# S4 convolution times SwiGLU gate on one core: the last two output tiles finished in column halves, their stores on two queues, and the fill of ones put first in the list

## The chip, the core and the metric

One core of one Trainium2 chip. The metric is device microseconds of one execution; a kernel's time is the median of its runs. The kernel before ran three times: 611.83, 613.95 and 614.11 us, median 613.95 us.

## What is computed

The input u has L = 2048 rows of D = 512 columns. It is normalised by row, and from the normalised rows come an S4 convolution over time and a SwiGLU feed-forward network, whose SiLU gates the convolution:

```python
xn = _layernorm(x)                       # x = A_u, (1, 2048, 512)
P  = exp(logdA[:, :, None] * l)          # (512, 128, 2048), complex
K  = einsum("dn,dnl,dn->dl", Cc, P, dB).real
s  = irfft(rfft(xn padded to 4096) * rfft(K padded)) + xn * Dskip
g  = silu((silu(xn @ w_gate) * (xn @ w_up)) @ w_down)     # 512 -> 1792 -> 512
return x + s * g
```

## The kernel before: tasks, a list and a planner

**Tasks.** The kernel is written as 1,964 small tasks. Each call of `add` (line 141) describes one: an engine, a planned duration, a function that emits its instructions, and the buffers that it reads and writes. `LIST` (line 47) is a fixed permutation of the tasks, two characters for each; it is the order in which they are emitted, and so the order of every engine's in-order queue. Loads are issued by SP, most stores to the output by ACT.

**The planner.** `Plan.run` (line 177) walks the list and gives each task a planned start and end from planned durations. It does not change the order. From the planned times come three things. Buffers in on-chip memory get an address in one arena of 118 KB per partition (`place`, line 289): two buffers may share bytes if their planned lives do not meet, and the later one's first writer then waits in fact for the earlier one's last reader. PSUM banks are picked by the earliest planned release. And `keep_warm` (line 254) puts fill matmuls (line 1423) of a constant tile of ones into the PE queue where PE would stand idle by plan: a gap from s to e is filled with `int((e - s - 0.2) * 0.8 / 0.213)` of them, in front of the task that ends the gap; the first gap begins at a fixed 1.5 us. A fourth thing is `part_ports` (line 243), which adds a wait between a DVE task and a later POOL task that the plan puts within 8 us of each other.

**The start.** The first rows of x are loaded in 128-row tiles (`rows_in`, L489), the weights in seven column chunks for each of gate, up and down (`w_load`, issued at L468). A chunk's squares are summed on ACT (L604), cast to the row `hsq` on DVE (L614), summed over partitions by a matmul with the tile of ones (L615), and turned into a scale on DVE (L635 to L639). With the scale ACT makes the f16 high part of the chunk (L669) and DVE the low part (L670). A tile of x has its statistics on DVE (L503), is centred and scaled on ACT (L529, L530), its low part made on DVE (L531), is transposed on PE (L540) and copied from PSUM on DVE (L546). Then the first feed-forward matmuls can run (L699; down projection L741). The first stage of the transform of x is L563, copied by ACT (L567). The constant of ones, with a column of pi/2, is written by the DVE task at L474; before the change it stands 15th in the list, and fifth among DVE's tasks, behind two tiles' statistics, the Newton steps of the reciprocal root and the first `hsq`.

**The end.** `final` (line 1292) finishes the output: for a pair of tiles and one half of the columns it loads the transformed product (L1305, issued at L468), the rows of x (L1309) and the stored gate, does the last matmul (L1324), multiplies by the gate on DVE (L1333), adds x on POOL or, for the last tiles, DVE (L1336, L1338), and ACT stores two 64-row halves (L1340). The last two tiles, 14 and 15, are done singly over all 512 columns; their gate comes straight from the down projection: ACT's SiLU (L748) of a 128x512 PSUM bank.

ACT's queue at the end of the list before, in order: a store of pair 0/1, one of pair 4/5 and one more of 0/1, the two of tile 14 with the two of pair 12/13 (seven stores, between the SiLU of tile 14 and that of tile 15); then the SiLU of tile 15, the two stores of pair 2/3, the two of pair 6/7 and the two of tile 15.

Of the kernel before, what the change touches and what calls it, by code (L numbers as in the profile page):

```python
# [13 lines left out]
I32 = mybir.dt.int32  # L14
AF = mybir.ActivationFunctionType
# [14 lines left out]
NB = 8  # L30
# [17 lines left out]
    "#)#(#'#K#&#%#J#L#.#T#i#M#N#k###l#/#O#U#R#j#m#V#n#1#v#P#2#Q#S#D#Y#4#W#-#X#Z#5#+#w#o#x#y#q#,#p#r#*&+#8#z(*#s#t&.(+"  # L48
# [9 lines left out]
    ".M)e.G%]..)X.-./.L.N*$.X.Q.S.O.P%Z.R)Y)Z.T%[.0.1)m%a._.`%d.f)y'')n.b.3.U.2)z)f)[)o*%){)g%X%i'1.[.^.l.m)h*&.Y)p.a"
    "*'.o*()v.V**.c.|.Z)q%b.])|)r.i.k.n.p.g.h.}/#/$*..j%^/%%e*1)}/&/'/(*#%j.d.q.r%c.s*2//*3%k*)*:%n%f*/%g%s.t&{*0.v%_"
    "/).u*;*+*B*4*C.w%h.x.y.z.{/*/+%o%p*</,/./-*6*D*E/5%t/6/0%q/1/3*,/7%l*-/2/D*5*F*7/8/:/Q/9/>&|%m%r&)*G/</4*>/;/S%u"  # L60
    "*8/@*9%v*=*?/=';/?/E*L&'*M/F/H'%/G*@%w*H*A/R/j/I/k/l/M*N*P*I*J/J/O/K/L*K/i*O%y/N'&/A/B*Q*T*U*V*]/Z/]*X/T/V/X/Y'("
    "*R/[/m/n')/U'**S/W'</P/^*W/C/o/p'2/_*Y*Z'3'=/q*[*h%x/}'+/r/s/`*^'4'5/t/u*o/v*e'E'F'G/a*f*g*i',/c/d'T/e%z&#'6'/%{"
    "/b/f/h/g/y&$*j'9'7*_/{%|'-*k*l'.0U&%*a01/w/x0#&&%}&*/z'>*`*b'?0$'H'I*p0%02*c*q*d*m0&0>*n0+/|0:0<&(0V*w0(0?0X0W0'"
    "*x0Z+$0)+%0[0-*r030*0,'U050B0D0G0Y0^07040I0@0A0C'V0.+.0]'00806'J'M090;0E+/*s0_'@0F0`'N0H*t0/00':'K0=0J0a'S'Y'A'B"
    "+&+''C'D+0*u*v0b0K*y0L0n0c0d0e0g0h0i0k+1+60f*z1/0j0M'q0l0Q'L0p0O0o'Z'O0P0N1#*{0u0v0m+(0r0t0R0S0w0}100q0s*|+)1$+*"
    "0T0y*}+#++0x1G+21H1)1*'R'P1F1J+31K1L1,1I+7+81%1'0z+,+-+:1+1-+4+51315'W181:+911+;12141&1(0{0|'{1617+I19+>+<1M'Q1Q"
    "+=1T1U1O+?+@+A1N'81.'X'['g1[1W']1;1<1P1=+F+G1R'|'}+B+C1>1B1Z1V'^'_1]1^1S1x+D1X1@1_'r'h's'i1A+P1j+Q+X+Y1b1a+a+b't"
# [53 lines left out]
class Plan:  # L121
# [55 lines left out]
    def run(self):  # L177
        order = [self.tasks[i] for i in LIST]
        free = dict.fromkeys(("PE", "DVE", "ACT", "POOL", "SP"), 0.0)
# [3 lines left out]
        dma_free = port_free = 0.0  # L183
# [209 lines left out]
def kernel(  # L393
# [73 lines left out]
    def load(dst, src, names, size, pieces, pr, rd=(), ahead=None):  # L467
        add("SP", 0.4, lambda: sy.dma_start(dst(), src), up=names, rd=rd, pr=pr, dma=dma_us(size, pieces), root=True, ahead=ahead)  # L468
# [260 lines left out]
    def down(b, t, c, hh, pos):  # L729

        idx = (b * 2 + t) * NC + c
        if c == 0:
            zps[b, t] = bank(f"z{b}{t}", "p")
        z = zps[b, t]

        def mm():
            h = hh.view(F16).rearrange("p (l n) -> p l n", l=2)
            w = wt["d"][:, c].rearrange("p l (i d) -> p l i d", i=2)
            for i in range(2):
                for k, (hl, wl) in enumerate(((0, 0), (0, 1), (1, 0))):  # L740
                    T.matmul(z.t, h[:, hl, i * 256 + t * P:i * 256 + (t + 1) * P], w[:, wl, i],  # L741
                             start=(c == 0 and i == 0 and k == 0), stop=(c == NC - 1 and i == 1 and k == 2))
        add("PE", 1.3, mm, rd=[hh, key(f"wd{c}")], wr=[z], up=[key(f"down{idx}")], pr=ffn_due(pos) + W["dn"],
            slack=SLD if b == t == 0 else 0.0)
        if c == NC - 1:
            j = 2 * b + t
            zg = zgs[j] = buf(f"zg{j}", 2048, "zg" if b < ZK else None, 2)
            add("ACT", 0.69, lambda: S.activation(zg.f32(), z.t, AF.Silu, scale=zsc[:, 1:2]), rd=[z], wr=[zg], c=1, pr=0)  # L748
# [7 lines left out]
    def prep(hf):  # L756
# [395 lines left out]
    def kg_s1(i):  # L1152
# [109 lines left out]
    def s2_inv(m, c):  # L1262
# [17 lines left out]
        for q in range(4):  # L1280
# [8 lines left out]
            add("SP", 0.4, lambda q=q, b=b: sy.dma_start(bs_d[c, m, q].rearrange("k p d -> p k d"), b.f32().rearrange("p (k d) -> p k d", k=2)),  # L1289
                rd=[b], up=[key(f"bs{c}")], c=0, dma=dma_us(262144, 256))  # L1290

    def final(js, cs, c):
# [33 lines left out]
        add("PE", 0.92 if nj == 2 else 1.06, mm, rd=[bt, key("j2")], wr=[py], c=2, pr=pr, f32=6)  # L1326
        ot = buf(f"ot{tag}", 2048, "ot", int(W["c_ot"] + 0.5))
# [24 lines left out]
    add("SP", 0.4, lambda: sy.dma_start(ldt, log_dt.rearrange("(c p) -> p c", p=P)), up=[key("ldt")], pr=18, dma=0.7)  # L1352
# [4 lines left out]
    for k in range(2):  # L1357
        add("SP", 0.4, lambda k=k: sy.dma_start(dsk[k * 64:k * 64 + 64].rearrange("(f r) d -> f r d", r=2)[:, k], dskip.partition_broadcast(32)),
# [112 lines left out]
```

## Time and profile before

| | |
|---|---|
| three runs | 611.83, 613.95, 614.11 us; median 613.95 |
| the profiled execution | 610.76 us; its span 609.0 us, so 1.76 us lie around the span |
| PE busy | 581.9 us, 96% of the span |
| DVE, ACT, POOL busy | 432.3, 342.1, 326.2 us |
| moved by DMA | 93.10 MB |

Times in the views are microseconds from the start of the span. A line of the timeline gives start, duration, engine, source line, operation, tiles and shapes, how often it came in a row, and in brackets how long the engine had stood idle and what released it. PE is the matmuls, PEld the weight loads beside them; SPq and ACTq are DMA issues on those engines' queues.

### The profile page before, as it was taken

How to read it: one execution, taken by the hardware profiler on the slowest of the kernel's cores; microseconds unless marked ns; L12 is line 12 of the kernel's file. 1: busy time of each engine (PE TensorE's matmuls, PEld its weight loads, DVE VectorE, ACT ScalarE, POOL GpSimd, SP SyncE). 2: the span in 40 equal slices, each digit the busy share in tenths (PEclk: the TensorE clock that was granted, in tenths of full speed). 3: DMA queues.
4: the chain of work that ended last, by engine and by line, in shares of the span. 5: the costliest groups of instructions: out<-in, count | busy, mean ns of one | idle time of the engine just before them, and what ended most of it. 6: DMA issues, size and time to landing. Idle time of an engine off the chain costs nothing.

```text
span 609.0 us, 18323 instructions
## 1 busy us (share of the span) xinstructions
PE 581.9 (96%) x7625; PEld 411.6 (68%) x7625; DVE 432.3 (71%) x988; ACT 342.1 (56%) x697; POOL 326.2 (54%) x301
## 2 busy tenths in 40 slices
PE   4999999999999999999999999999989999999974
PEld 1678886556888678766787677776657656667531
DVE  3777989665798989888779876878848556673313
ACT  5689856655765468667778687746632423131100
POOL 0145522279974768649997799688023341530131
PEclk9999999999999999999999999999989999999978
DMA  8699621024004041025340123556969889999997
GB/s 261 167 286 321 196 79 48 1 97 155 16 3 95 4 113 37 2 68 169 114 110 15 30 79 138 172 129 172 320 180 275 265 246 270 270 286 255 222 265 184
DMA packets 100594, 93.10 MB, mean 153 GB/s; under 512 B 38496, under 2 KB 83808, under 8 KB 100512
## 3 DMA queue, kind: packets, MB, share of 16 engines
q1 hardware_dynamic: 96000, 87.48, 50.0%
q10 hardware_dynamic: 4512, 4.46, 2.8%
q8 instruction: 60, 0.98, 0.7%
q14 instruction: 22, 0.18, 0.1%
HBM read 59.02 MB, written 32.90 MB: 151 GB/s over the span
## 4 chain that ended last, share of the span: by engine, by line
PE 84%; DMA 9%; DVE 3%; issue 1%; ACT 1%; SPq 0%; ACTq 0%; POOL 0%; DVEq 0%; POOLq 0%
PE p L699 45%; PE p L741 21%; PE p L1145 5%; DMA out_dram<-arena 3%; PE p L1230 3%; PE p L1237 2%; DMA arena<-zg_d 2%; DMA arena<-in_A_u_dram 2%; PE p L1277 2%; PE p L563 2%; PE p L1423 2%; PE p L1178 1%; DMA arena<-bs_d 1%; PE p L540 1%; DMA wd<-in_B_w_gate_dram 1%
## 5 line engine op out<-in xcount | busy, mean ns | idle before, releaser
L699 PE MATMUL p<-arena,wu 128*128 128x256 f16 x1344 | 157.3, 274 | 4.0 <-issue 4.0
L741 PE MATMUL p<-wd,arena 128*128 128x512 f16 x672 | 155.4, 381 | 0.0
L699 PE MATMUL p<-arena,wg 128*128 128x256 f16 x1344 | 155.2, 273 | 0.0
L699 PEld LDWEIGHTS <-wu 128*128 128x128 f16 x1344 | 130.7, 98 | 26.9 <-issue 8.8
L699 PEld LDWEIGHTS <-wg 128*128 128x128 f16 x1344 | 129.7, 98 | 23.0 <-issue 3.7
L741 PEld LDWEIGHTS <-arena 128*128 128x128 f16 x672 | 63.5, 98 | 77.1 <-issue 9.3
L1078 POOL TENSOR_TENSOR arena<-arena 128x1536 f32<-128x1536 f32 x32 | 90.7, 2840 | 18.0 <-DVE arena L854 5.6
L720 ACT ACTIVATE arena<-p,inv 128x512 f32<-128x512 f32 x56 | 38.4, 689 | 65.4 <-PE p L699 57.1
L1070 POOL TENSOR_TENSOR arena<-arena 128x1024 int32<-128x1024 int32 x32 | 62.4, 1955 | 18.5 <-DVE arena L830 7.5
L722 DVE SCALAR_TENSOR_TENSOR p<-p,shc,arena 128x512 f32<-128x512 f32 x56 | 42.2, 754 | 30.1 <-PE p L699 17.8
L724 ACT CAST arena<-p 128x512 f16<-128x512 f32 x56 | 32.5, 589 | 33.8 <-DVE p L722 16.4
L1113 DVE TENSOR_TENSOR arena<-arena,p 128x512 f32<-128x512 f32 x64 | 43.6, 681 | 8.4 <-ACT p L1094 6.4
L1336 POOL TENSOR_TENSOR arena<-arena 128x512 f32<-128x512 f32 x12 | 15.1, 1268 | 57.7 <-DMA arena<-in_A_u_dram 37.9
L725 DVE TENSOR_TENSOR arena<-p,arena 128x512 f16<-128x512 f32 x56 | 37.7, 683 | 11.2 <-ACT arena L724 11.2
L1094 ACT ACTIVATE p<-p,halfpi 128x512 f32<-128x512 f32 x64 | 42.4, 664 | 1.4
L1093 ACT ACTIVATE p<-arena 128x512 f32<-128x512 int32 x64 | 38.9, 610 | 6.4 <-DVE arena L1185 2.2
L1095 ACT ACTIVATE p<-arena 128x512 f32<-128x512 int32 x64 | 37.5, 602 | 8.7 <-DVE arena L1115 4.5
L1259 POOL TENSOR_TENSOR arena<-arena 128x512 f32<-128x512 f32 x16 | 20.3, 1275 | 38.5 <-DVE arena L1255 14.1
L1260 POOL TENSOR_TENSOR arena<-arena 128x512 f32<-128x512 f32 x16 | 20.3, 1272 | 31.3 <-DVE arena L1255 17.8
L1119 DVE SCALAR_TENSOR_TENSOR arena<-arena,p 128x256 f32<-128x256 f32 x64 | 26.5, 414 | 12.6 <-ACT p L1095 8.9
L1145 PEld LDWEIGHTS p<-arena 128*32 128x32 f32 x2048 | 29.7, 110 | 6.6 <-issue 4.2
L1145 PE MATMUL p<-arena 128*32 128x64 f32 x2048 | 33.4, 220 | 0.0
(180 smaller groups left out, 814.0 us busy)
## 6 DMA issues: line engine op xcount, KB each, us to landing
ax_d<-arena SPq DMA_DIRECT2D x32, 256.0 KB, 2.6
ak_d<-arena SPq DMA_DIRECT2D x16, 512.0 KB, 6.5
arena<-ak_d SPq DMA_DIRECT2D x16, 512.0 KB, 5.7
arena<-ax_d SPq DMA_DIRECT2D x16, 512.0 KB, 6.7
bs_d<-arena SPq DMA_DIRECT2D x32, 256.0 KB, 4.8
arena<-in_A_u_dram SPq DMA_DIRECT2D x62, 128.0 KB, 5.0
arena<-in_B_w_down_dram SPq DMA_DIRECT2D x14, 512.0 KB, 6.0
arena<-bs_d SPq DMA_DIRECT2D x14, 512.0 KB, 8.5
```

What stands on the lines that cost most here:

```text
L699: T.matmul(pg.t[:, i * 256:(i + 1) * 256].rearrange("p (a t) -> p a t", a=2), w[:, wl, d, i * P:(i + 1) * P], x[:, :, xl, d, :], start=(k ...
L720: add("ACT", 0.69, lambda: S.activation(sg.f32(), pg.t, AF.Silu, scale=inv[:, c, 0:1]), rd=[pg], wr=[sg], c=1, pr=e)
L722: add("DVE", 0.75, lambda: V.scalar_tensor_tensor(pu.t, pu.t, shc[:, c:c + 1], sg.f32(), op0=ALU.mult, op1=ALU.mult), rd=[sg], wr=[pu], c= ...
L725: add("DVE", 0.7, lambda: V.tensor_tensor(hh.view(F16)[:, 512:1024], pu.t, hh.view(F16)[:, 0:512], op=ALU.subtract), rd=[pu], wr=[hh], c=1 ...
L741: T.matmul(z.t, h[:, hl, i * 256 + t * P:i * 256 + (t + 1) * P], w[:, wl, i], start=(c == 0 and i == 0 and k == 0), stop=(c == NC - 1 and ...
L1070: G.tensor_tensor(a, h_[:, :, :, None].to_broadcast([P, 2 * GT, 4, 8]), l_[:, :, None, :].to_broadcast([P, 2 * GT, 4, 8]), op=ALU.add)
L1078: G.tensor_tensor(e, p_[:, :, :, None].to_broadcast([P, 3 * GT, 4, 8]), q_[:, :, None, :].to_broadcast([P, 3 * GT, 4, 8]), op=ALU.mult)
L1093: add("ACT", 0.62, lambda: S.activation(tc_.t, a(), AF.Abs, scale=SIN_SCALE), rd=[an], wr=[tc_], pr=pr)
L1094: add("ACT", 0.7, lambda: S.activation(tc_.t, tc_.t, AF.Sin, bias=halfpi, scale=-1.0), rd=[key("ones")], wr=[tc_], c=4, pr=pr)
L1095: add("ACT", 0.62, lambda: S.activation(ts.t, a(), AF.Sin, scale=SIN_SCALE), rd=[an], wr=[ts], pr=pr + 0.2)
L1113: V.tensor_tensor(o[:, :, 0:64].rearrange("p d (s j) -> p d s j", s=2), e[:, :, 0:64].rearrange("p d (s j) -> p d s j", s=2), t[:, :, None ...
L1145: T.matmul(kt[h * 32:(h + 1) * 32, (r * GD + dd) // 4], o[:, ri, dd + h, 64:96], o[:, ri, dd + h, 0:64], start=(ri == 0), stop=(ri == 1), ...
```

## The change

The list of the kernel after, read task by task against the one before, differs in two places only; every other task keeps its place on its engine, though nearly all characters differ, as ten new tasks shift the numbers.

1. The task that writes ones and pi/2 (L474) moves from the 15th place to the first.
2. For tiles 14 and 15 the SiLU is two tasks of 256 columns, into two buffers of 1 KB per partition; the product and the sum are two tasks of 256 columns each; and each column half is stored in two 64-row DMAs of 64 KB, the first on SP, the second on ACT. DVE does product, product, sum, sum. The seven stores on ACT between the two SiLUs are now: pair 0/1, pair 4/5, tile 14 twice, 0/1, 12/13 twice; the six behind the SiLU of tile 15: 2/3 twice, tile 15 twice, 6/7 twice. The four stores on SP stand last in SP's queue.

Apart from that the planner's figures change: engines start at 0.7 instead of 0, the DMA engines at 1.2, and an issue on SP counts 0.52 us instead of 0.4. These set planned times, and through them addresses, banks and the number of fills.

```diff
-        free = dict.fromkeys(("PE", "DVE", "ACT", "POOL", "SP"), 0.0)
+        free = dict.fromkeys(("PE", "DVE", "ACT", "POOL", "SP"), 0.7)
...
-        dma_free = port_free = 0.0
+        dma_free, port_free = 1.2, 0.0
...
-        add("SP", 0.4, lambda: sy.dma_start(dst(), src), up=names, rd=rd, pr=pr, dma=dma_us(size, pieces), root=True, ahead=ahead)
+        add("SP", 0.52, lambda: sy.dma_start(dst(), src), up=names, rd=rd, pr=pr, dma=dma_us(size, pieces), root=True, ahead=ahead)
...
+            if b == NB - 1:
+                zgs[j] = [buf(f"zg{j}{q}", 1024) for q in range(2)]
+                for q in range(2):
+                    add("ACT", 0.44, lambda q=q: S.activation(zgs[j][q].f32(), z.t[:, q * HD:(q + 1) * HD], AF.Silu, scale=zsc[:, 1:2]), rd=[z], wr=[zgs[j][q]], c=1, pr=0)
+                return
...
+        if nj == 1:
+            for q, z in enumerate(zgs[j0]):
+                ot = buf(f"ot{tag}{q}", 1024, "ot")
+                sl = slice(q * HD, (q + 1) * HD)
+                add("DVE", 0.42, lambda ot=ot, z=z, sl=sl: V.tensor_tensor(ot.f32(), py.t[:, sl], z.f32(), op=ALU.mult), rd=[py, z], wr=[ot], c=1, pr=pr)
+                add("DVE", 0.42, lambda ot=ot, sl=sl: V.tensor_tensor(ot.f32(), ot.f32(), fx.f32()[:, sl], op=ALU.add), rd=[fx], wr=[ot], c=1, pr=pr, port=True)
+                for h in range(2):
+                    add(("SP", "ACT")[h], 0.6, lambda h=h, ot=ot, sl=sl: (sy, nc.scalar)[h].dma_start(ov[h, :, j0, sl], ot.f32()[h * 64:(h + 1) * 64]),
+                        rd=[ot], up=[key("out")], c=0, dma=dma_us(65536, 64), pr=pr)
+            return
```

More of the change, by code (lines that the diff above doesn't have):

```diff
@@ L47 @@
 LIST = (
-    "#)#(#'#K#&#%#J#L#.#T#i#M#N#k###l#/#O#U#R#j#m#V#n#1#v#P#2#Q#S#D#Y#4#W#-#X#Z#5#+#w#o#x#y#q#,#p#r#*&+#8#z(*#s#t&.(+"
+    "###)#(#'#K#&#%#J#L#.#T#i#M#N#k#l#/#O#U#R#j#m#V#n#1#v#P#2#Q#S#D#Y#4#W#-#X#Z#5#+#w#o#x#y#q#,#p#r#*&+#8#z(*#s#t&.(+"
     "#]&/(,(.#}$&#7#[$'$(${(/$)#C#d#;#{#^&0#|$#(0#e(4#_#`&E#f%S&3$*#g&,#a$+#h#b#c(-#:$$(1$-#<&5$w&v(5$2&:&8$x(6$z$y$,"
@@ L58 @@
[L58 to L67, printed above, removed]
@@ L83 @@
-    "8?8k8l8m"
+    "&I&a)%%G%H&G&L%I%;&H(s&V&K%J&M%L)1)2%M)3):%K%@%4-H%1)I&N&O&Q&P)R)S&W)&)J%N&b-I-M);(t&<)<-N&T)T&2)U)'(u&X#G-O&l(v"
+    "&c%O&Y%W&m)])^&w'#&R-J&n&p&o&[-K&q&d&f&i&e&])_&S-L-P)`&_-Q&z&^&Z)b-T)*&`)K&s&t'$)i)j-R%V-S-U&g&h&j-^-b-_&U-W-X-Z"
+    "-m)k)l)s)t-n)c)+-z-e-Y-[-V-f)@-`-a)B-d-c-{.7#H)a-g-i&-)d-h)A-v-x.8),.#.%&r-q-s.9-]-j)--o-p-r.6)4)6-t%U-u).)/)L.:"
+    ".;)C.<.=-w.&-k-l.')5)7-|-})w.$.(.*.))8)9.>-y)D.D)E.Y.E.G.F.H)u.+.,.-)N.K)V)M.A.C%Y)O.?.@.B.J)W)P)x%`)Q#F...g.L.M"
+    ".O)e.I%].0)X./.1.N.P*$.Z.S.U.Q.R%Z.T)Y)Z.V%[.2.3)m%a.a.b%d.h)y'')n.d.5.W.4)z)f)[)o*%){)g%X%i'1.^.`.n.o)h*&.[)p.c"
@@ new lines @@
+    "*'.q*()v.X**.e/#.])q%b._)|)r.k.m.p.r.i.j/$/%/&*..l%^/'%e*1)}/(/)/**#%j.f.s.t%c.u*2/1*3%k*)*:%n%f*/%g%s.v&{*0.x%_"
+    "/+.w*;*+*B*4*C.y%h.z.{.|.}/,/-%o%p*</./0//*6*D*E/7%t/8/2%q/3/5*,/9%l*-/4/F*5*F*7/:/</S/;/@&|%m%r&)*G/>/6*>/=/U%u"
+    "*8/B*9%v*=*?/?';/A/G*L&'*M/H/J'%/I*@%w*H*A/T/l/K/m/n/O*N*P*I*J/L/Q/M/N*K/k*O%y/P'&/C/D*Q*T*U*V*]/]/_*X/V/X/Z/['("
+    "*R/^/o/p')/W'**S/Y'</R/`*W/E/q/r'2/a*Y*Z'3'=/s*[*h%x0$'+/t/u/b*^'4'5/v/w*o/x*e'E'F'G/c*f*g*i',/e/f'T/g%z&#'6'/%{"
+    "/d/h/j/i/{&$*j'9'7*_/}%|'-*k*l'.0W&%*a03/y/z0%&&%}&*/|'>*`*b'?0&'H'I*p0'04*c*q*d*m0(0@*n0-0#0<0>&(0X*w0*0A0Z0Y0)"
@@ new lines @@
+    "*x0]+$0++%0^0/*r050,0.'U070D0F0I0[0`09060K0B0C0E'V00+.0_'00:08'J'M0;0=0G+/*s0a'@0H0b'N0J*t0102':'K0?0L0c'S'Y'A'B"
+    "+&+''C'D+0*u*v0d0M*y0N0p0e0f0g0i0j0k0m+1+60h*z110l0O'q0n0S'L0r0Q0q'Z'O0R0P1%*{0w0x0o+(0t0v0T0U0y1$120s0u*|+)1&+*"
+    "0V0{*}+#++0z1I+21J1+1,'R'P1H1L+31M1N1.1K+7+81'1)0|+,+-+:1-1/+4+51517'W1:1<+913+;14161(1*0}1#'{1819+I1;+>+<1O'Q1S"
+    "+=1V1W1Q+?+@+A1P'810'X'['g1^1Y']1=1>1R1?+F+G1T'|'}+B+C1@1D1]1X'^'_1_1`1U1z+D1Z1B1a'r'h's'i1C+P1l+Q+X+Y1d1c+a+b't"
+    "+E1A1E(#'`1e1g'j1G1y+J'k1m'a1u1f+L($1h+K+c1b26271[1i+M1n'u1o1q'b1{+R+T251w292:+N1|+O2#2'2)281p2;1r1F+S1s+k+d1t'c"
@@ new lines @@
+    "'l1v2%2&2('d1j+Z+U2<'e'o'm2='p+V2I+W1}2$2@1k'n2>2B2?+]+l+[+^2C1x'f2D2*2E2X+H2F(%+_2J(&((+e2K2L2f2A2G2`'v2+'y('+s"
+    "'w+`'x2a'z2N2M2O2Y2Z2H+g2c+f+h2P2g3#()+t2R2T+m2Q2[2S+i2]2^2b2,2d+j4`2U2}+n3j2_+u2-2V2W+{2/3l+v3w2o2q3k2j2l+o3y2e"
+    "2.2h21202i3&3'3(222m2n+p+q2p+w2k3m3n3o2r3x3$3%3)+r3z3{+x3p3t+y2337+z3|+|3}3+3,3-3s3*3r,(2s4#4$3q3u4&4%+}4'3v,#24"
+    "4(,)2t32,$303/3.2u34,*,12x48,%2w2y2v2z36,&,'4)312{,+334-4.43443S3:353<3?2|3E3=453>3@4E384C,2,9393;3R,-46473A3B3F"
+    ",3,J4*,:,A,B,,404+41423G3H,.3L3J3M3C3D3O4/3T3U4^3W3[3^3Y3Z3]3N3P4D4_,4,/,03I3K4,3V3X4k49,C4:4F4<4m4;4@5*4G4H4?4>"
@@ new lines @@
+    "3Q3_4=4A3`3a4l4a4b59575+4I4K4M4L4J,53b3f4O4c4d3e58,64N3c4n3d3g,73i,84o4p4B4g,;,<4f4P4Z4T4W,=4U,D4Q3h5,,E4X4R4h4Y"
+    "4q4e4[,>4V,?4u4]4r,F4j6+5:4t4s4w5<4i,@,G5=5;4v6,5{5-5/5@6G5>506-5.54525y5?5A535B516E,K5C,L5z,N,M,O4x4y4z555$5%4|"
+    "4}5Q4S5'5(6F,P5)56,H,Q,I,R,S,T5a5|5S6$,U5}5_6#6(6&6%6'6)5#5&6.606H6J,Z616n6*6/63656264,V,W,[6I6S4{5b6o,X,Y6K6L66"
+    "6O6N6M5d675T6m,]6z5U5`5D,^5N5O5K5L6Q5E6P5F,c6|5P6T,d,e5H5I,l5c5G5e5f5h5i5g5j5M6p6q6r,_,`5J5R686?6@6<6B6C6R7K6=,f"
+    "7a,m79696:5k6U6s6v6u6w6t6y7r,g6D7O6x,t,u6A7D5W5V5X5Z5Y5[5]6>6W5^6;6{7<6X6V6Y6Z,a7;,|6]7_,}7E7B7N6[6_6^,b,h7:6}7$"
@@ new lines @@
+    "7#7^7=7h7%7>,n-#7?7T7g7),o7(7L7C7M5l5s,p5m7&7'7+7*7`7A,i7p5n7W7P5v,v5w5p7@5o,j,k5t5q5r7q,w5x7,767F7G5u7V7i737Q74"
+    "7H777875,x7-6`7.,y7/7U70716d6e6g726j6k6a6b6f6l6c7b7c7d6h6i7S,q-*-+7f7J-$-&7R7e-,8K80,z-.8B7j,r7y8'8C,{,s-%-'8_8N"
+    "8)7z-(-2-3-4-58T8O7|8M8P-68L898E7s8k---)-/-7-0837X8U7Y7Z848D-1-:7u8V7t7v-8-97{8`8^8l7l818a827k7m8Q7o7n8R8<7w7[8("
+    "7I8*8F8G8H8I8J8n858S7]8W-?7}8;8X8#7x8:86888m-;8$-<-=->-@8=8&8b8c8g878d8f8h8j8e8i8%8Y8Z8+8,8-8]8[8>-A-B-C-D-E-F-G"
+    "8.8/8o8p8t8q8s8u8w8r8v8?8@8A"
@@ L567, in x_stage1 @@
             add("ACT", 0.6, lambda h=h, xa=xa: S.copy(xa.f32(), pa[h].t), rd=[pa[h]], up=[xa], c=5 if j < 4 else 2, pr=pr)
-            add("SP", 0.4, lambda h=h, xa=xa: sy.dma_start(ax_d.rearrange("f r t d -> (f r) t d")[:, 2 * j + h], xa.f32()),
+            add("SP", 0.52, lambda h=h, xa=xa: sy.dma_start(ax_d.rearrange("f r t d -> (f r) t d")[:, 2 * j + h], xa.f32()),
                 rd=[xa], up=[key("ax")], c=0, dma=dma_us(262144, 128))
@@ L749, in down @@
             if b < ZK:
-                add("SP", 0.4, lambda: sy.dma_start(zg_d[j], zg.f32()), rd=[zg], up=[key(f"zgd{j}")], c=0,
+                add("SP", 0.52, lambda: sy.dma_start(zg_d[j], zg.f32()), rd=[zg], up=[key(f"zgd{j}")], c=0,
                     dma=dma_us(262144, 128))
@@ L914, in prep @@
                 w_ = o[k].size // 4
-                add("SP", 0.4, lambda k=k, off=off, w_=w_: sy.dma_start(kp_d[:, off:off + w_], o[k].view(I32)),
+                add("SP", 0.52, lambda k=k, off=off, w_=w_: sy.dma_start(kp_d[:, off:off + w_], o[k].view(I32)),
                     rd=[o[k]], up=[key("kpd" + k)], c=0, dma=dma_us(262144, 128))
@@ L1288, in s2_inv @@
             add("DVE", 0.87, both, rd=[pb[q]], wr=[b], c=1, pr=e)
-            add("SP", 0.4, lambda q=q, b=b: sy.dma_start(bs_d[c, m, q].rearrange("k p d -> p k d"), b.f32().rearrange("p (k d) -> p k d", k=2)),
+            add("SP", 0.52, lambda q=q, b=b: sy.dma_start(bs_d[c, m, q].rearrange("k p d -> p k d"), b.f32().rearrange("p (k d) -> p k d", k=2)),
                 rd=[b], up=[key(f"bs{c}")], c=0, dma=dma_us(262144, 256))
@@ L1351 @@
             w_load(nm, c)
-    add("SP", 0.4, lambda: sy.dma_start(ldt, log_dt.rearrange("(c p) -> p c", p=P)), up=[key("ldt")], pr=18, dma=0.7)
+    add("SP", 0.52, lambda: sy.dma_start(ldt, log_dt.rearrange("(c p) -> p c", p=P)), up=[key("ldt")], pr=18, dma=0.7)
     c_load("f1x", f1x_t, f1x, 2.6)
@@ L1357 @@
     for k in range(2):
-        add("SP", 0.4, lambda k=k: sy.dma_start(dsk[k * 64:k * 64 + 64].rearrange("(f r) d -> f r d", r=2)[:, k], dskip.partition_broadcast(32)),
+        add("SP", 0.52, lambda k=k: sy.dma_start(dsk[k * 64:k * 64 + 64].rearrange("(f r) d -> f r d", r=2)[:, k], dskip.partition_broadcast(32)),
             wr=[key(f"dsk{k}")], rd=[key("dsk")], pr=61, dma=0.5)
```

21 lines of the change are left out of this document (1 added, 20 removed).

## The prediction

> **What bounds the kernel now.** I read the page first, then the chain that ended last in order of time, then the timelines of its two ends.
>
> ```profile
> span 609.0 us, 18323 instructions
> PE   4999999999999999999999999999989999999974
> PE 84%; DMA 9%; DVE 3%; issue 1%; ACT 1%; SPq 0%; ACTq 0%; POOL 0%; DVEq 0%; POOLq 0%
> ...
> 34.99 5.35 PE p L699 x48
> ...
> 540.66 1.04 PE p L1324 x8
> 547.34 3.17 DMA arena<-in_A_u_dram
> ...
> 595.05 2.80 DMA out_dram<-arena
> ```
>
> The chain has three parts: a start up to about 35 us, over 500 us in which almost every link is a matmul, and from 547 us a drain by DMA. The middle is a rigid block: its order is a list that the change leaves alone. So two questions matter: by how much earlier does the block begin, and what is saved behind it?
>
> ```profile
> 8.76 0.16 DVE L614 CAST hsq<-ssq 128x1 bf16<-128x1 f32 x1
> 8.89 0.17 DVE L474 MEMSET ones<- 128x128 bf16 x1
> 9.11 8.10 PE L1423 MATMUL p<-ones 128*128 128x512 bf16 x27 [9.11 <-DVE halfpi L474]
> 10.12 0.75 DVE L531 SCALAR_TENSOR_TENSOR arena<-arena,rstd 128x512 f16<-128x512 f32 x1 [1.06 <-ACT arena L530]
> 13.21 1.06 ACT L604 ACTIVATE wu<-wd 128x1024 bf16<-128x1024 f32 x1 [0.43 <-DMA wd<-in_B_w_up_dram]
> 14.17 0.19 ACT L604 ACTIVATION_READ_ACCUMULATOR wu<-wd 128x1 f32 x1
> 17.05 0.17 PE L615 MATMUL p<-hsq,ones 128*128 128x1 bf16 x1
> 17.26 0.16 DVE L635 TENSOR_SCALAR ssq<-p 128x1 f32<-128x1 f32 x1 [6.38 <-PE p L615]
> 17.64 1.15 ACT L669 ACTIVATE wg<-wd,scw 128x1024 f16<-128x1024 f32 x1 [3.28 <-DVE scw L624]
> ```
>
> The start hangs on one thing. The sum of squares of the first gate chunk lies ready at 8.92, but its matmul L615 runs at 17.05, because 27 fills stand before it in PE's queue and could not begin until 9.11, when the constant of ones was written. DVE idles 6.38 us for it, ACT 3.28. Work meant to fill idle time has become the wait.
>
> **Part 1: ones first.**
>
> ```profile
> 0.24 0.10 POOL L1456 MEMSET const-float32-0.0<- 128x1 f32 x1 [0.24 <-issue]
> 0.74 0.41 SPq L468 DMA_DIRECT2D idh_t<-in_idh_dram  x1
> ```
>
> The memset needs nothing. POOL's earliest memset runs at 0.24 and SP's first issue at 0.74, so DVE's will run between those; I take 0.74. From the memset's start to the first fill the rows give 0.22, so the fills start at 0.96 and 27 of them end at 9.06. The planner now starts its clocks 0.7 to 1.2 us later, which by its own formula adds up to 1.2 x 0.8 / 0.213 = 4 fills; at the mean of the 27 (0.30) the end is at most 10.3. So L615 runs between 9.1 and 10.3. Next late on DVE is L531, standing before L635 and done at 10.87, which covers that spread. L635 goes from 17.26 to about 10.9: DVE gains 6.4 us there. That is not yet the gain of the kernel; I follow what binds next.
>
> ```profile
> 10.61 0.60 SPq L489 DMA_DIRECT2D arena<-in_A_u_dram  x1
> arena<-in_A_u_dram SPq DMA_DIRECT2D x1, 128.0 KB, 8.5
> 20.37 0.16 DVE L614 CAST hsq<-ssq 128x2 bf16<-128x2 f32 x1
> 20.62 0.15 DVE L624 TENSOR_SCALAR scw<-ssq 128x1 int32<-128x1 int32 x1
> 20.87 1.15 ACT L669 ACTIVATE wu<-wd,scw 128x1024 f16<-128x1024 f32 x1 [2.09 <-DVE scw L624]
> 20.89 1.28 DVE L670 SCALAR_TENSOR_TENSOR wg<-wd,scw,wg 128x1024 f16<-128x1024 f32 x1
> 22.62 1.27 DVE L670 SCALAR_TENSOR_TENSOR wu<-wd,scw,wu 128x1024 f16<-128x1024 f32 x1
> 23.81 0.69 DVE L503 BATCH_NORM_STATS2 st<-arena 128x6 f32<-128x512 f32 x1
> ```
>
> - ACT keeps its order: L669 of the gate chunk comes behind the squares that wait for the load of the second up chunk, and those end at 13.21 + 1.06 = 14.27. It starts at 14.27 instead of 17.64 (3.4 earlier) and ends at 15.42.
> - ACT's second L669 (20.87) needs the scale from L624. The cast at 20.37 that stands before it needs the sum of the same squares, read out by 14.17 + 0.19 = 14.36; 20.62 + 0.15 - 20.37 = 0.40 later the scale is there, by 14.8. So ACT itself binds: 15.42, a gain of 5.4.
> - DVE's L670 of the gate chunk needs the first L669: 15.45 instead of 20.89, 5.4 earlier; the second (22.62) follows at 17.2 and ends at 18.45.
> - Then L503 wants the next tile of x. Its half was issued at 10.61 and takes 8.5 to land: 19.1. These loads are first in SP's queue in the same order as before, and nothing here speeds them. L503 goes from 23.81 to 19.1: **4.7 us earlier**.
>
> From here on everything that I followed (the scales, L529 and L530 of these tiles, the next chunks, PE's L699) hangs on work that is 4.7 to 5.4 us earlier; the smaller counts. Does it stay?
>
> ```profile
> 30.00:35.00 5.00, 3.91 (x43) 2.62 (x41) 3.07 (x8) 4.97 (x8) 3.95 (x2) 1.00 0.98 283
> 75.00:80.00 5.00, 5.00 (x48) 4.49 (x47) 3.77 (x7) 1.27 (x2) 2.81 (x2) 1.00 0.01 3
> ```
>
> The columns are the window's length, busy time of PE, PEld, DVE, ACT and POOL, the granted clock, DMA share and GB/s. DMA is nearly full from 30 to 35 us, which could swallow the gain, but at 75 it is idle and PE still full: loads come from then on as work frees their buffers, and move with it. So the block, and the drain behind it, shift by 4.7.
>
> **Part 2: the last two tiles.**
>
> ```profile
> 597.05 0.69 ACT L748 ACTIVATE arena<-p,zsc 128x512 f32<-128x512 f32 x1 [23.53 <-DMA arena<-in_A_u_dram]
> 597.13 4.70 ACTq L1340 DMA_DIRECT2D out_dram<-arena  x7
> 601.88 0.69 ACT L748 ACTIVATE arena<-p,zsc 128x512 f32<-128x512 f32 x1 [4.14 <-DMA out_dram<-arena]
> 602.29 3.93 ACTq L1340 DMA_DIRECT2D out_dram<-arena  x6
> 602.76 0.69 DVE L1333 TENSOR_TENSOR arena<-p,arena 128x512 f32<-128x512 f32 x1 [1.25 <-PE p L1324]
> 603.49 0.69 DVE L1338 TENSOR_TENSOR arena<-arena 128x512 f32<-128x512 f32 x1
> L1333 DVE TENSOR_TENSOR arena<-p,arena 128x256 f32<-128x256 f32 x8 | 3.1, 417 | 4.9 <-PE p L1324 4.9
> L1287 ACT COPY arena<-p 128x256 f32<-128x256 f32 x8 | 2.5, 383 | 4.5 <-PE p L1277 4.5
> ```
>
> The end is ACT's queue: SiLU, seven issues of 0.67 us, SiLU, six of 0.66, and one store's landing. The change leaves seven and six on ACT: SP gets four stores that did not exist. So the queue that ends last is not relieved. A half SiLU costs between the 0.383 of a 128x256 copy and 0.69; I take 0.45, so two cost 0.9 instead of 0.69, but the issue at 597.13 lies inside the SiLU already, and the extra 0.2 is hidden where issues wait for data. DVE's four halves at 0.417 are 1.67 instead of 1.38, yet the first product starts 0.24 sooner: the second sum ends where the whole one did. New waits on ACT: tile 14's stores now stand before a store of pair 0/1, the two of 12/13 and the last SiLU; their data comes by about 599.2, when ACT would issue them anyway. Tile 15's stores can go at about 603.7, before those of 6/7, and may fill a short hole. The four on SP have nothing behind them. Sum: 0.1 gained, with bounds of 1.3 gained (two issues, were they off the path) and 0.5 lost (both SiLU splits and a DVE half on it).
>
> **Part 3: the new planned times.** They move addresses, banks and added waits, with no row that shows the effect. The nearest are waits of SP for a buffer still being read:
>
> ```profile
> SPq L468 <- PE p L1277: 3.6, 1, 3.6
> SPq L468 <- PE p L1324: 3.3, 2, 2.7
> ```
>
> Such a wait may vanish or appear: -3.6 to +3.6 for one. In the middle PE seldom waits for anything, so I take nothing and keep the ends for the range.
>
> **The sum.** 4.7 + 0.1 = 4.8 us. Against the profiled execution, 609.0 of span and 610.76 in all, that gives 604.2 and 606.0. The median of the runs is 3.19 above that execution, and I carry that over: 613.95 - 4.8 = **609.2 us**, 0.8% faster. About 0.5% (3.07 us) is what a measurement can tell from no change.
>
> **Rivals.**
>
> *Absorbed.* The start moves but the gain is lost where DMA is full: from 25 to 60 us the loads come late and PE waits for weights, or the drain holds the end. For it: the share 0.98 in the window above. Against: the 0.01 at 75. It also covers the case that the fills are not freed, say because more of them are planned than I reckon. Time 612 to 614. Chance 0.23.
>
> *More.* If the tile of x lands sooner than 19.1, the next limit is ACT's 5.4, and with both stores off the path at the end 1.3: 613.95 - 6.7 = 607.3. Chance 0.12.
>
> *Slower: addresses.* In the drain every load waits for a free buffer. If the new addresses put several of them on buffers that are in fact read late, SP's in-order queue stands still. One such wait costs 3.6; to turn the gain into a loss of over 0.5% takes more than 4.8 + 3.07 = 7.9 us, that is three on the path: 609.2 + 10.8 = 620. Chance 0.07.
>
> *Cold PE.* The fills now end 8 us sooner, and PE may cool before its first real block.
>
> ```profile
> 440.00:460.00 20.00, 17.33 (x300) 12.54 (x279) 10.93 (x24) 5.84 (x14) 5.07 (x5) 0.91 0.71 199
> 444.01 4.07 PE L699 MATMUL p<-arena,wu 128*128 128x256 f16 x23 [2.67 <-issue]
> ```
>
> An idle 2.67 us shows up beside a granted clock of 0.91 over 20 us, that is 20 x 0.09 / 0.5 = 3.6 us at half clock. If that struck at 15.4, the first 24 L699 (2.8 us) would take 5.6, and the gain falls by up to 2.8, to 612.0. By my walk PE's longest idle piece after the fills is under 1 us (fills and transposes up to 14.3, L615 at 14.6, L563 to 15.4, then L699). Chance 0.03. The Trainium skill, "TensorE: Matmul & The Clock Gate", section "Part 1: The HAM clock gate", says that the array falls to half rate after at least one idle window of about 3.4 us and returns after about as long of sustained work; by that rule nothing would cool here. The idle piece in the trace is shorter than that window, so the row is the stricter of the two.
>
> **How the numbers follow.** My forecast has 0.55, "more" 0.12, absorbed 0.23, slower 0.07, cold 0.03. Faster by over 0.5% (under 610.9): 0.55 + 0.12 = 0.67. Within: 0.23 + 0.03 = 0.26. Slower by over 0.5% (above 617.0): 0.07. The range goes from 605.3 ("more", less 2 for a buffer wait that vanishes) to 613.0, which takes in cold and half of absorbed.
>
> **What would show it.** Right: the first fill near 1 us; L615 near 9 to 10; L635's wait on it gone; ACT's first L669 near 14.3; L503 (the third tile) near 19 and ended by the load of x; the long run of L699 starting 4.7 before 34.99; the same number of ACT issues at the end, about 0.65 each. Wrong: PE idle for weights between 25 and 60 us; an end that does not move with the block; a new wait of SP for a buffer in the drain; L503 still waiting for anything but the load.

## The result, and the profile after

| | before | after |
|---|---|---|
| median of 6 runs each | 613.67 us | 609.42 us (607.22 to 610.26) |
| ratio of the two | | 0.9926 [0.9905, 0.9947] |
| the profiled execution | 610.76 us, span 609.0 | 608.71 us, span 606.9 |

The change makes the kernel 0.74% faster: 4.25 us between the medians, 3.3 to 5.8 by the interval. Predicted were 609.2 us and a gain of 4.8. The two profiled executions differ by only 2.05 us, because that of before lay 2.9 us under its median and that of after 0.7 under. The traces are read for places, the medians for the size.

The page of after, and the chain that ended last in order of time (start, duration, what):

```profile
span 606.9 us, 18342 instructions
PE   8899999999999999999999999999899999999873
PE 83%; DMA 10%; issue 2%; SPq 2%; DVE 1%; ACT 1%; POOL 0%; POOLq 0%; ACTq 0%; DVEq 0%
```

```profile
30.64 5.35 PE p L699 x48
...
536.97 1.04 PE p L1329 x8
...
553.24 8.18 DMA arena<-bs_d
...
598.04 3.42 issue
```

It is the same three-part chain. The block begins at 30.64 instead of 34.99, 4.35 earlier. The last matmul of this line before the drain stands at 536.97 against 540.66 (3.69 earlier), and the span is shorter by 2.1. So in this pair a part of the shift is gone behind the block: 0.86 between that matmul and the SiLU of tile 14 (57.25 us for 56.39), and 0.7 at the end, which is read below. The timelines of the start, PE first, then DVE, then ACT:

```profile
1.05 7.94 PE L1438 MATMUL p<-ones 128*128 128x512 bf16 x29 [1.05 <-DVE halfpi L474]
9.92 0.16 PE L615 MATMUL p<-hsq,ones 128*128 128x1 bf16 x1 [0.93 <-DVE hsq L614]
...
0.83 0.17 DVE L474 MEMSET ones<- 128x128 bf16 x1 [0.83 <-PEq L1471]
9.71 0.16 DVE L614 CAST hsq<-ssq 128x1 bf16<-128x1 f32 x1 [1.60 <-ACT wg L604]
11.75 0.15 DVE L635 TENSOR_SCALAR ssq<-p 128x1 f32<-128x1 f32 x1
15.85 1.28 DVE L670 SCALAR_TENSOR_TENSOR wg<-wd,scw,wg 128x1024 f16<-128x1024 f32 x1 [0.43 <-ACT wg L669]
19.70 0.70 DVE L503 BATCH_NORM_STATS2 st<-arena 128x6 f32<-128x512 f32 x1 [0.84 <-DMA arena<-in_A_u_dram]
...
14.69 1.14 ACT L669 ACTIVATE wg<-wd,scw 128x1024 f16<-128x1024 f32 x1
15.72 1.14 ACT L669 ACTIVATE wu<-wd,scw 128x1024 f16<-128x1024 f32 x1
```

The fills now run in PE's empty time, and PE now waits for `hsq`, where before the matmul of `hsq` waited for PE. The wait of 6.38 us in front of L635 is gone. In its place stands the one foretold: L503 waits for the load of the third tile of x, and its bracket names that DMA.

The end, on ACT, DVE and POOL:

```profile
594.22 0.47 ACT L750 ACTIVATE arena<-p,zsc 128x256 f32<-128x256 f32 x1 [26.58 <-DMA out_dram<-arena]
599.46 0.47 ACT L750 ACTIVATE arena<-p,zsc 128x256 f32<-128x256 f32 x1 [4.39 <-DMA out_dram<-arena]
601.16 1.37 ACTq L1339 DMA_DIRECT2D out_dram<-arena  x2
602.79 1.30 ACTq L1355 DMA_DIRECT2D out_dram<-arena  x2
...
600.67 0.75 DVE L1337 TENSOR_TENSOR arena<-arena 128x256 f32<-128x256 f32 x2
...
601.50 1.26 POOL L1351 TENSOR_TENSOR arena<-arena 128x512 f32<-128x512 f32 x1 [2.29 <-DVE arena L1337]
```

and POOL's sums at the end of before:

```profile
600.99 2.49 POOL L1336 TENSOR_TENSOR arena<-arena 128x512 f32<-128x512 f32 x2 [8.11 <-DVE arena L1333]
```

From the SiLU of tile 14 to the end of ACT's last issue it is 604.09 - 594.22 = 9.87 us. Before it was 602.29 + 3.93 - 597.05 = 9.17. The halves thus cost 0.70 here instead of gaining 0.1. The two POOL rows show where to look: before, POOL did both its last sums in one run; now the second waits 2.29 us for DVE's last sum of tile 15. That POOL sum writes the row of pair 6/7, whose two stores are the last in ACT's queue.

### The profile page after: what moved, and what is told of

The parts are those of the page before. It is cut to its first block, busy times and chain, and to the rows that moved or that the text cites. A ratio compares the mean times of both kernels' runs of the same rounds, so it can differ in the third digit from the quotient of the medians.

```text
span 606.9 us, 18342 instructions
## 1 busy us (share of the span) xinstructions
PE 582.9 (96%) x7628; PEld 411.4 (68%) x7628; DVE 433.1 (71%) x992; ACT 342.3 (56%) x699; POOL 326.7 (54%) x301
## 4 chain that ended last, share of the span: by engine, by line
PE 83%; DMA 10%; issue 2%; SPq 2%; DVE 1%; ACT 1%; POOL 0%; POOLq 0%; ACTq 0%; DVEq 0%
PE p L699 45%; PE p L741 21%; PE p L1150 5%; DMA out_dram<-arena 3%; DMA arena<-in_A_u_dram 3%; PE p L1242 3%; PE p L1235 3%; DMA arena<-zg_d 2%; PE p L1282 2%; PE p L563 2%; PE p L1183 1%; DMA arena<-bs_d 1%; SPq L468 1%; PE p L540 1%; DMA wd<-in_B_w_up_dram 1%
## 5 line engine op out<-in xcount | busy, mean ns | idle before, releaser
L699 PE MATMUL p<-arena,wu 128*128 128x256 f16 x1344 | 155.6, 273 | 0.3 <-issue 0.3
L699 PE MATMUL p<-arena,wg 128*128 128x256 f16 x1344 | 155.4, 273 | 0.3 <-DVE wg L670 0.3
L699 PEld LDWEIGHTS <-wg 128*128 128x128 f16 x1344 | 129.6, 98 | 23.6 <-issue 3.3
L699 PEld LDWEIGHTS <-wu 128*128 128x128 f16 x1344 | 130.2, 98 | 22.0 <-issue 4.7
L1075 POOL TENSOR_TENSOR arena<-arena 128x1024 int32<-128x1024 int32 x32 | 62.4, 1956 | 19.1 <-DVE arena L835 7.5
```

The lines of the kernel that those rows point to most:

```text
L699: T.matmul(pg.t[:, i * 256:(i + 1) * 256].rearrange("p (a t) -> p a t", a=2), w[:, wl, d, i * P:(i + 1) * P], x[:, :, xl, d, :], start=(k ...
L1075: G.tensor_tensor(a, h_[:, :, :, None].to_broadcast([P, 2 * GT, 4, 8]), l_[:, :, None, :].to_broadcast([P, 2 * GT, 4, 8]), op=ALU.add)
```

## The experiments

The theory: all of the gain comes from the 27 fills that no longer stand ahead of L615; the block then begins about 10.95 us after L503, which the load of x holds, and the rest moves with it. Rivals: PE's clock, raised earlier by fills that start at 1 us; the planner's figures; the halves at the end. Each kernel is set beside runs of before on the same chip; ratios are to those.

**One part at a time.** The ones first, alone, in before:

```diff
-    "#)#(#'#K#&#%#J#L#.#T#i#M#N#k###l#/..."
+    "###)#(#'#K#&#%#J#L#.#T#i#M#N#k#l#/..."
```

> The kernel before with the task of ones (L474) put first in the list and nothing else: old planner figures, whole last tiles. If the gain is the first scale matmul L615 freed from the 27 fills ahead of it, the whole gain is here: 4.0 to 4.7 us under before, L615 at 9 to 10 us, the third tile's statistics L503 near 19.5 and waiting for the load of x. If the new planned times or the halves of the last tiles make the gain, this one is within 1 us of before.

Before 614.17 us, this 608.93: ratio 0.9904 [0.9869, 0.9939]. Its chain and DVE's timeline:

```profile
30.45 5.35 PE p L699 x48
```

```profile
19.50 0.69 DVE L503 BATCH_NORM_STATS2 st<-arena 128x6 f32<-128x512 f32 x1 [0.75 <-DMA arena<-in_A_u_dram]
```

One memset moved by 14 places gives the whole gain, with the same wait for x. The halves alone, in after:

```diff
-    "###)#(#'#K#&#%#J#L#.#T#i#M#N#k#l#/..."
+    "#)#(#'#K#&#%#J#L#.#T#i#M#N#k###l#/..."
...
-        free = dict.fromkeys(("PE", "DVE", "ACT", "POOL", "SP"), 0.7)
+        free = dict.fromkeys(("PE", "DVE", "ACT", "POOL", "SP"), 0.0)
...
-        dma_free, port_free = 1.2, 0.0
+        dma_free = port_free = 0.0
```

and every 0.52 of an SP issue back to 0.4.

> The kernel after with the task of ones back in the 15th place and the old planner figures: what is left is the last two tiles in column halves with stores on both queues. If ACT's queue of issues ends the kernel and keeps its number of issues, 0.1 us gained, between 1.3 gained and 0.5 lost. If two queues for the stores make the gain, 2 to 4 us under before.

614.17, ratio 0.9988 [0.9957, 1.0019]: no change outside the interval. Its chain, then DVE and PE at the start and ACT at the end:

```profile
36.12 5.35 PE p L699 x48
```

```profile
9.40 0.16 DVE L614 CAST hsq<-ssq 128x1 bf16<-128x1 f32 x1 [1.06 <-ACT wg L604]
9.75 8.59 PE L1438 MATMUL p<-ones 128*128 128x512 bf16 x27 [9.75 <-DVE halfpi L474]
...
600.62 0.47 ACT L750 ACTIVATE arena<-p,zsc 128x256 f32<-128x256 f32 x1 [23.97 <-DMA out_dram<-arena]
609.23 1.30 ACTq L1355 DMA_DIRECT2D out_dram<-arena  x2
```

Its end takes 610.53 - 600.62 = 9.91 us from the SiLU to ACT's last issue, as in after. All six profiles, here and below, that have the halves with their stores and sums in this order show 9.86 to 9.91, the four with whole tiles 9.15 to 9.23. So the 0.7 belongs to the halves; the interval of the time, 2.6 us faster to 1.2 slower, is too wide to show it. The planner's figures alone are the reverse of these last edits, in before:

> The kernel before with the planner's new figures alone (engines from 0.7, DMA from 1.2, 0.52 an issue on SP): the same list, so only addresses, banks, added waits and the number of fills change. If these don't matter, within 1 us of before, L615 as late as before or up to 1 us later (more fills ahead of it). If the new addresses make the gain, about 4 us under before.

614.25, ratio 1.0008 [0.9978, 1.0038]: nothing.

```profile
9.47 8.93 PE L1423 MATMUL p<-ones 128*128 128x512 bf16 x30 [9.47 <-DVE halfpi L474]
```

```profile
36.17 5.34 PE p L699 x48
```

They plan three fills more (30 for 27), and that is all that the start shows. These two kernels also tell how far the start varies while the ones are written late. Their blocks begin at 36.12 and 36.17, not at 34.99 as in the profiled execution of before. In plan_only the fills began 0.36 later and the 30 took 0.83 longer than the 27; tail_only has the same 27 fills as before, and its rows say why it is later: `hsq` stood ready 0.64 us later (9.40 for 8.76) and the fills took 0.49 longer (8.59 for 8.10), which makes the 1.13. With the ones late, the start hangs on the landing of the first gate chunk and then on the fills' time; with the ones first it began at 30.64, 30.45 and 30.70 in three profiles. So the shift is 4.35 from the start of before and 36.1 - 30.6 = 5.5 from that of tail_only; which is the typical one, two profiles can't tell.

**Fills or clock.** In before, the first gap begins at 9.1 instead of 1.5, so that the fills ahead of L615 vanish while the ones stay late (no result changes):

```diff
-WARM_FROM, WARM_SPAN, WARM_IDLE, WARM_SHARE, WARM_DUR = 1.5, 3.4, 1.0, 0.8, 0.213
+WARM_FROM, WARM_SPAN, WARM_IDLE, WARM_SHARE, WARM_DUR = 9.1, 3.4, 1.0, 0.8, 0.213
```

> The kernel before with the first gap's 27 fills left out (the gap begins at 9.1 in the plan instead of 1.5); the constant of ones is written as late as before, the later fills stay, and no result changes. If the fills ahead of L615 are the cost, L615 runs at about 9.1 to 9.3 and the time falls as with ones first, 3.5 to 4.7 us under before, though PE is at half clock for its first 3 to 4 us. If the gain comes from a PE that is warm sooner, there is none here: within 1 us of before or slower.

609.05, ratio 0.9898 [0.9846, 0.9951]: the full gain without the change. PE and DVE at the start:

```profile
9.96 0.19 PE L615 MATMUL p<-hsq,ones 128*128 128x1 bf16 x1 [9.96 <-DVE halfpi L474]
10.01 2.30 PE L1423 MATMUL p<-ones 128*128 128x512 bf16 x5
14.58 1.46 PE L1423 MATMUL p<-ones 128*128 128x512 bf16 x6
...
19.89 0.69 DVE L503 BATCH_NORM_STATS2 st<-arena 128x6 f32<-128x512 f32 x1 [0.94 <-DMA arena<-in_A_u_dram]
```

PE begins cold: its first five fills take 2.30 us, 0.46 each, where six at 14.58 take 1.46, 0.24 each. The Trainium skill, "TensorE: Matmul & The Clock Gate", section "Part 1: The HAM clock gate", has full rate come after about one window of 3.4 us of work; 10.01 to 14.58 agrees with that roughly. The kernel pays nothing for it: L503 still waits for x, and the block begins at 30.84, 10.95 after L503, as in after (30.64 - 19.70 = 10.94). So the gain does not come from a PE that is warm sooner, and fills that run cold there cost nothing.

More fills push the other way. In after, the first gap's fills times two, and times three (no result changes):

```diff
-            n = int((e - s - 0.2) * WARM_SHARE / WARM_DUR)
+            n = int((e - s - 0.2) * WARM_SHARE / WARM_DUR) * (2 if s == WARM_FROM else 1)
```

> The kernel after with twice as many fills in the first gap (29 to 58, no result changes). If what counts is how long L615 stands behind fills, and DVE's and ACT's own work covers the first part of it: the fills end at 1.05 + 7.94 + 29 x 0.216 = 15.3, L635 moves from 11.75 to 15.5, the third tile's L503 from 19.7 to about 22.2, and the time rises by 2.5 us over after, still some 2 us under before. If the whole delay of 6.3 us counted: 6.3 over after, slower than before. If the fills' place in the queue doesn't matter: as after.

610.9, ratio 0.9942 [0.9909, 0.9976].

```profile
1.05 14.32 PE L1438 MATMUL p<-ones 128*128 128x512 bf16 x58 [1.05 <-DVE halfpi L474]
...
15.45 0.16 DVE L635 TENSOR_SCALAR ssq<-p 128x1 f32<-128x1 f32 x1 [3.50 <-PE p L615]
```

The old wait on L615 is back, and the block begins at 33.36, 2.7 later than in after. The time rises by about 1 us by the ratios, with intervals that overlap; this alone decides nothing.

> The kernel after with three times the fills in the first gap (87 instead of 29, no result changes). With twice as many the long block of matmuls began 2.7 us later; now nothing covers the further 29 fills, so it begins another 6.3 us later, near 39.7 us. If a later block moves the end one for one: 9 us over after, 3 to 4 us over before. If the drain by DMA sets the end and swallows the shift: within 3 us of after.

613.39, ratio 0.9986 [0.9968, 1.0004]. The same kernel as after, run again beside it:

> The kernel after once more, as the reference on the same chip for the three beside it: 0.990 to 0.995 of before.

610.25, ratio 0.9928 [0.9901, 0.9954]: after holds its gain on another chip. The chain of the threefold kernel:

```profile
39.91 5.35 PE p L699 x48
...
457.78 5.35 PE p L699 x48
...
542.24 1.04 PE p L1329 x8
```

The block moved as expected, by 39.91 - 30.64 = 9.27. But the time rose by 3.1 only, not by 9. The chains say where the shift goes: 9.27 at the start of the block, 7.12 at the L699 of 457.78 (450.66 in after), 5.27 at the last L1329 (536.97 in after). The groups of PE between 400 and 500 us, busy time, mean ns and idle time before them, first of after, then of the threefold:

```profile
L1242 PE MATMUL p<-arena 64*32 64x256 f32 x331 | 12.6, 379 | 2.7 <-issue 2.7
L1150 PE MATMUL p<-arena 128*32 128x64 f32 x256 | 4.5, 220 | 1.3 <-issue 1.3
```

```profile
L1235 PE MATMUL p<-arena 64*32 64x256 f32 x416 | 14.7, 379 | 0.5 <-issue 0.5
L1242 PE MATMUL p<-arena 64*32 64x256 f32 x352 | 12.9, 378 | 0.4 <-issue 0.4
```

PE stands for 4.0 us in after while the profile names nothing that it waits for; the threefold kernel has 0.9 of that. These 3.1 us are most of the 4.0 (9.27 - 5.27) lost up to the last L1329, in this pair of profiles. In the profile of after_again the same places stand at 30.70, 450.71 and 539.94, so against it the shift goes from 9.21 to 7.07 and then to 2.30: there PE waits 1.99 us at 529.46 for ACT's L1292, which waited for a load, and the 48 L699 behind that take 7.07 us instead of 5.40.

What PE stands for without a name, the traces do show. The page of after, and two rows of PE:

```profile
q8 instruction: 60, 0.98, 0.7%
```

```profile
435.77 1.20 PE L1150 MATMUL p<-arena 128*32 128x64 f32 x67 [1.35 <-issue]
...
440.05 0.62 PE L1242 MATMUL p<-arena 64*32 64x256 f32 x4 [1.21 <-issue]
```

By the page q8 brings instructions, in 60 packets of 16 KB: one for each 127 of the 7,628 matmuls with their weight loads. The two pauses lie 67 + 32 + 28 = 127 matmuls apart, and both fall inside a run of like matmuls. The 14 traces hold 46 pauses of PE over 0.2 us between 25 and 545 us for which no releaser is named, and each of them ends 1.2 to 1.6 us after a packet of q8 has landed. They stand at the same count and not at the same task: behind 5,574 recorded matmuls comes an L1242 in after and an L1235 in the threefold kernel, and PE pauses before both. So there PE waits for its own instructions. The 1.99 us of after_again lie at such a place too, a packet landed 1.5 us before their end; there the load and the instructions can't be told apart.

Each fill more moves the cuts between blocks to an earlier task. That this is why the threefold kernel stands less fits, but no run tests it, and more fills don't mean fewer pauses: between 400 and 500 us before has 4.0 us of them, after_again 3.6, the twofold kernel 3.8 and no_first_fills 1.4 (and 1.0 just ahead of 400). The way from start to end is no straight line either: with the ones late a block at 36.1 goes with 614.2 us (tail_only, plan_only), and here one at 39.9 with 613.4.

**Beyond the limit.** If the load of x binds L503, loading it sooner should shift the start further. In after, SP issues the loads of the third and fourth tile of x ahead of the third up chunk, and ACT takes that chunk's squares behind the tile's L529; these are moves in the list alone.

```diff
-...#S#D#Y#4#W#-#X#Z#5#+#w#o#x#y#q#,#p#r#*&+...
+...#S#D#Y#4#W#-#,#+#*#X#Z#5#w#o#x#y#q#p#r&+...
...
-...#[$'$(${(/$)#C#d...
+...#[${(/#C#d$'$($)...
```

> The kernel after with the loads of the third and fourth tile of x moved ahead of the third up chunk's load in SP's queue, and that chunk's squares moved behind the third tile's L529 on ACT. If the landing of x is what limits the start now: L503 from 19.7 to about 18.9 with no wait on DMA, and 0.5 to 0.9 us under after. If ACT or the chunk's scale is as late: within 0.3 us of after.

608.81, ratio 0.9926 [0.9891, 0.9961]. DVE and ACT:

```profile
18.34 0.69 DVE L503 BATCH_NORM_STATS2 st<-arena 128x6 f32<-128x512 f32 x1
...
20.95 1.13 ACT L669 ACTIVATE wg<-wd,scw 128x1024 f16<-128x1024 f32 x1
```

L503 no longer waits for a DMA and runs 1.4 earlier, but ACT's L669 of the next gate chunk starts at 20.95 (21.27 in after), and the block at 30.34: 0.3 won. What binds now is ACT: right before that L669 it has the squares that the edit put there, from 19.91 to 20.95. So 0.3 is what this edit wins; no run moved the load of x without the squares.

**The end.** Two suspects for the 0.7: the issues on ACT, and POOL's sum behind the halves. First all eight half stores of the last two tiles on SP, in after:

```diff
-                    add(("SP", "ACT")[h], 0.6, lambda h=h, ot=ot, sl=sl: (sy, nc.scalar)[h].dma_start(...
+                    add("SP", 0.6, lambda h=h, ot=ot, sl=sl: sy.dma_start(...
```

> The kernel after with all eight half stores of tiles 14 and 15 on SP, so that ACT issues five and four stores at the end instead of seven and six. If ACT's issues of about 0.65 us each end the kernel: the second SiLU 1 us sooner, the last issue on ACT some 2 us sooner, the end then on SP, 1.0 to 2.0 us under after. If the end is held by DMA or by the products instead: within 0.5 us of after.

609.57, ratio 0.9940 [0.9908, 0.9972], no gain over after outside the interval. ACT and POOL:

```profile
598.49 0.47 ACT L750 ACTIVATE arena<-p,zsc 128x256 f32<-128x256 f32 x1 [25.36 <-DMA out_dram<-arena]
603.07 0.84 ACT L750 ACTIVATE arena<-p,zsc 128x256 f32<-128x256 f32 x2 [3.75 <-DMA out_dram<-arena]
603.51 4.19 ACTq L1355 DMA_DIRECT2D out_dram<-arena  x4
...
605.12 1.26 POOL L1351 TENSOR_TENSOR arena<-arena 128x512 f32<-128x512 f32 x1 [1.64 <-DVE arena L1337]
```

Between the two SiLUs ACT has five issues instead of seven, and saves 0.66: 4.58 us against 5.24 in after. Behind the second, four issues end 607.70 - 603.07 = 4.63 later, exactly as long as the six of after (604.09 - 599.46 = 4.63): the last two wait for POOL, and POOL for DVE. The Trainium skill, "DMA: Bandwidth & Descriptors", section "Issuing engines are not separate DMA queues", says that issuing from several engines saves only the time to issue; this end agrees, and behind the second SiLU not even that is saved, as the data come late.

Then POOL's last sum and its two stores ahead of tile 15's sums in the list, in after:

```diff
-    "8.8/8o8p8t8q8s8u8w8r8v8?8@8A"
+    "8.8/8o8p8t8?8@8A8q8s8u8w8r8v"
```

> The kernel after with POOL's last sum (pair 6/7) and its two stores put ahead of tile 15's sums in the list, as they stood in the kernel before. In the profile of after that POOL sum waits 2.29 us for DVE's last sum, by the wait that keeps the two engines' ports apart. If that wait is on the end's path, POOL ends 1 us sooner and the last issue on ACT comes 0.6 to 1.0 us sooner: 0.5 to 1 us under after. If not, as after.

609.19, ratio 0.9917 [0.9894, 0.9941].

```profile
595.01 0.47 ACT L750 ACTIVATE arena<-p,zsc 128x256 f32<-128x256 f32 x1 [27.89 <-DMA out_dram<-arena]
603.15 1.20 ACTq L1339 DMA_DIRECT2D out_dram<-arena  x2
...
598.74 2.48 POOL L1351 TENSOR_TENSOR arena<-arena 128x512 f32<-128x512 f32 x2 [8.17 <-DMA out_dram<-arena]
```

POOL does both sums in one run again, and the end takes 604.35 - 595.01 = 9.34 us: 0.53 of the 0.70 is back. The edit also moves the two stores of 6/7 ahead of tile 15's on ACT; the two are not told apart. By medians the kernel is 1.06 under the run of after beside it; the intervals overlap, so the trace shows the wait gone and the time only points the same way.

Two combinations. The early x with the stores on SP:

> Stores on SP and x ahead, together, on top of after. If the one acts at the start and the other at the end, with a rigid block between them, the gains add: 1.5 to 2.9 us under after, about 607 us where before is at 614.

609.54, ratio 0.9924 [0.9889, 0.9959]: no gain over after outside the interval. In the trace POOL's last sum still waits 1.63 us for DVE. All three edits:

> On top of after: x ahead, the half stores on SP, and POOL's last sum ahead of tile 15's sums. Behind the second SiLU ACT has four stores that wait for POOL alone and SP has tile 15's: the last issue 2.5 to 3 us behind the second SiLU instead of 4.0, so 1.0 to 1.5 us at the end and 0.3 at the start under after. If the end is held by something else: within 0.5 us of after.

608.02, ratio 0.9895 [0.9858, 0.9931], the lowest of these kernels, but its interval overlaps that of after run beside it. ACT and SP:

```profile
596.88 0.47 ACT L750 ACTIVATE arena<-p,zsc 128x256 f32<-128x256 f32 x1 [25.19 <-DMA arena<-in_A_u_dram]
601.90 2.94 ACTq L1355 DMA_DIRECT2D out_dram<-arena  x4
...
598.55 7.28 SPq L1339 DMA_DIRECT2D out_dram<-arena  x8
```

ACT's last issue ends 604.84 - 596.88 = 7.96 after the first SiLU, 1.9 sooner than in after. Now SP's queue ends last, at 605.83, 8.95 after the SiLU, so 0.9 remains. Behind the second SiLU the stores on SP pay only with POOL's wait gone: 3.38 us there instead of 4.63.

## Why the prediction was right

- **What bounds the start: right.** The fills in front of L615 were the wait. Taking them away with the ones late gives 0.9898, moving the ones 0.9904, the whole change 0.9926.
- **Part 1, its steps.** First fill 1.05 (0.96 said), L615 9.92 (9.1 to 10.3), ACT's L669 14.69 and 15.72 (14.27 and 15.42), L670 15.85 (15.45), L503 19.70 and held by the load of x (19.1). L635 was the step farthest off among these, 11.75 for 10.9: the first gate chunk's `hsq` came at 9.71 where the profile of before had 8.76, and the ACT steps behind it were late too; L503 hid that. The block moved by 4.35 between the two profiles for 4.7 forecast, but by about 5.5 against the start of tail_only, so the term was too large by 0.35 or too small by 0.8, by the profile that one takes for before.
- **"The block, and the drain behind it, shift by 4.7": held here, and is no rule.** The time of ones_only fell by 3.7 to 8.0 us (614.17 times what its interval leaves of 1), which holds 4.35 and 5.5 alike. The threefold fills show that another 9.27 us of start costs only 3.1. The 0.01 of DMA at 75 us, on which the step rested, says that loads follow PE there; it says nothing of the stretch behind 400 us, where the lost part goes: in before the share is 0.94 from 420 to 440 us and 0.98 from 500 to 540.
- **Part 2: the step that failed.** "0.1 gained" was 0.70 lost in the traces, beyond the 0.5 of its bound. That ACT keeps its seven and six issues was right, as was the half SiLU (0.45 said, 0.47). What failed is the planned wait of POOL on DVE: the front part names that mechanism, and the new waits were gone through on ACT alone. POOL's last sum stood in the list behind tile 15's sums, and took the wait; pool_ahead, without it, has 0.53 of the 0.70 back, and the rest stays open.
- **Part 3: zero, as taken.** plan_only: 1.0008 [0.9978, 1.0038].
- **Rivals.** Absorbed: not for this change by the medians, but real for larger shifts. More: with the load of x sooner, ACT's work allowed 0.3 and not the 0.7 foreseen, in the one edit that tried it (x_early). Slower by addresses: plan_only shows no such thing. Cold PE: the granted clock of after is 1.00 from 14 to 20 us.

So the start, the mechanism that makes the gain, was foreseen and is shown. That 609.2 lies so near 609.42 is partly luck. The end was taken 0.8 too good, the start may have been taken up to 0.8 too small, and the median of before was itself 0.28 lower in the measurement than the 613.95 that the sum began with.

## What to carry to other kernels

A filler for idle time belongs behind nothing that arrives late and ahead of nothing that is needed: look in the trace for fills that begin when data come, and ask what stands behind them in that in-order queue. When a step has been freed, expect the next one close by: the load of x at 0.84 us of wait, and behind it ACT, which left 0.3 in x_early. When work at the end is split, list the waits of every engine whose last task now stands behind the split, not of the queue that issues the stores alone.

## What the runs showed of the hardware that was not expected

PE can stand still for its own instructions. Between 400 and 500 us it did so for 0.9 to 5.6 us in the 14 traces, at counts of matmuls that lie some 127, or a multiple of that, apart, and it went on 1.2 to 1.6 us after the next 16 KB had landed. The profile puts such pauses down to "issue". How much of a later start the kernel gives back stays open: by two profiles of one and the same kernel it is 4.0 or 6.9 of 9.2 us up to the last L1329. No kernel with the halves, the new figures and late ones was run, which would have set the whole change beside its start alone.
